# Clustered attention and an MLP on one core: row maxima over both halves of the keys at once, and PSUM divided anew

## The chip, the cores and the metric

The kernel runs on one core of a Trainium2 chip. A core has a matrix engine (TensorE, PE in the profile; PEld is its loading of weights), a vector engine (VectorE, DVE), a scalar engine (ScalarE, ACT), a general one (GpSimd, POOL) and queues for transfers (SP issues most of them, ScalarE's queue a few). Each engine takes its instructions in the order of the program and waits on semaphores. TensorE writes to PSUM, which has eight banks of 512 fp32 numbers for each of the 128 partitions, and VectorE and ScalarE read it there.

The metric is the device time of one execution in microseconds (us). Of the kernel before there are three runs, with a median of 1025.03 us (1023.77 to 1026.52). About 0.3% of that, 3.1 us, is what such a measurement can tell from no change.

## The reference

Attention within clusters for 4 batches and 8 heads, 768 positions of 64 numbers, then a mixing of positions of rank 32 and an MLP (512 to 2048 to 512), each with its residual:

```python
q_assign = np.argmax(np.einsum('bhsd,hcd->bhsc', q_n, c_n), axis=-1)
k_assign = np.argmax(np.einsum('bhsd,hcd->bhsc', k_n, c_n), axis=-1)
mask = q_assign[:, :, :, None] == k_assign[:, :, None, :]
scores = scale * np.matmul(q, k.transpose(0, 1, 3, 2))
scores = np.where(mask, scores, -1000000000.0)
scores = scores - np.max(scores, axis=-1, keepdims=True)
attn = np.exp(scores)
attn = attn / (np.sum(attn, axis=-1, keepdims=True) + 1e-09)
x = np.matmul(attn, v)            # heads side by side: (4, 768, 512)
...
xt = x.transpose(0, 2, 1)
h = xt @ U @ V
u = x + h.transpose(0, 2, 1)
ch = np.maximum(u @ w_ch1, 0.0) @ w_ch2
return (u + ch).astype(np.float32)
```

## The kernel before

Heads are worked in pairs: 16 of them (4 of each batch), j being the head within the pair. For a pair, queries and keys lie with their dimensions over the partitions, split into a high part (`X1`) and the rest (`X2`), so that two matmuls in a fast format give the accuracy of fp32. Below them stand 32 rows with the clusters, scaled so that a query and a key of different clusters get a huge negative score.

Stages of a pair:

- `load`, `split_hi`, `split_lo`, `place_*`: the transfers in, the split, and rows copied to the partitions where they are needed.
- `sims`, `largest`, `clusters`, `clusters_T`, `place_clusters`: similarities to the centroids (the tile `ps_sim`, turned into `ps_simT`), the largest of each row found on VectorE in five instructions that work in `ps_simT` itself, and the result turned (`ps_oh`) and placed.
- `rowmax`: for each unit u of 12 (a head and 128 queries), the scores of the high part against all 768 keys, in two halves h of 384. Each half is one matmul into a single bank (`ps_max`, L462) and one reduction on VectorE (L464) into a column of `m2`. `rowmax_T` (L469) takes the larger of the two halves for six or twelve units. `rowmax_place` turns the maxima (`ps_mT`), negates them on ScalarE (`mT`) and sends them by ScalarE's queue to a row of the queries' second part (row 96 of `X2`), where the matmul subtracts them.
- `scores`: for each of 12 steps (a half of the queries and 128 keys), four matmuls into the two banks of one tile `st`, one for each head (L500 with the high parts, L502 with the rest and the maxima), and one exponential over both (`pr`, L505).
- `weights`: the sums over keys, step by step, on GpSimd and some on VectorE (`T`, L515). `values`: six steps make a block of 12 matmuls (24 in the trace, which shows each of these in two) into one bank (`o_ps`, L523), which ScalarE copies out (`os`, L527).
- `sums`, `sums_T`, `normalise`: the sums over partitions, turned, and the outputs turned (`ps_oT`, L556) and divided.

After each four pairs `mix_u`, `mix_sum` and `mix_v` add the mix of positions (`mix_v`: one matmul into a bank named `ps_h`, L585, one addition on VectorE, L586, for each of six tiles). Beside all that, `load_weights` brings the weights, which come as 64-bit numbers, and joins them to fp32 on VectorE (L174 to L186; for the first two groups of them with a bank `ps_t` as the place of work). After the last pair the MLP runs in eight parts of 384 positions and 16 steps: `gemm1` (12 matmuls into `ps_h`), `gemm2` (9 into the three banks `y`).

The order is written out. `at(time, ...)` notes each piece of work with a time; times count in steps, 12 to a pair, and a piece's time is 12 i plus a number of the table `times`, with columns for most pairs, the last of a batch, the last, the first, the second and the third; `order0` holds those of the first pieces, and `spots` where the row maxima of six units stand within six steps. All are sorted by time and written in that order, which each engine keeps (`keep_order`). Which piece of a pool a tile gets follows from that order too; a tile waits until the one before it in its place has been read.

PSUM before: the pool `ps_w` has four single banks for everything short (`work`), the pool `ps_st` two tiles of two banks for the scores (and in the beginning for turned clusters). When the MLP begins, the four banks of `ps_st` become those of `y`.

Of the kernel before, what the change touches and what calls it, by code (L numbers as in the profile page):

```python
# [29 lines left out]
F32 = mybir.dt.float32  # L30
# [6 lines left out]
AX = mybir.AxisListType  # L37
# [16 lines left out]
GV = 6  # L54
# [5 lines left out]
    "load0":           (-34.72, -34.25, -43.39,   None,   None,  -24.6),  # L60
    "load1":           (-26.03, -29.07, -30.74,   None,   None,  -22.8),
    "sims":            ( -25.1, -28.59, -28.44,   None,   None, -21.52),
    "clusters_T":      (-19.38, -19.11, -17.83,   None, -12.09,  -13.9),
    "place_clusters":  (-18.31, -16.49, -15.63,   None, -10.17, -12.11),
    "split_hi0":       (-29.17, -30.23, -24.29,   None,   None, -20.71),
    "split_lo0":       (-24.63, -24.44, -24.29,   None,   None, -18.43),
    "split_hi1":       (-23.89, -23.69, -24.34,   None,   None, -19.53),
    "split_lo1":       (-23.65, -20.17, -23.57,   None,   None, -17.17),
    "place_keys_hi":   (-20.09, -23.65, -23.59,   None,   None, -17.07),
    "place_keys_lo":   (-19.84, -19.93, -21.77,   None,   None, -16.98),  # L70
    "place_queries":   (-16.28, -16.19, -18.28,   None,   None, -16.28),
# [5 lines left out]
    "scores":          (     0,  -0.97,  -0.37,  -0.47,   0.82,   0.95),
    "weights":         (  1.19,  -0.22,   0.44,   2.06,   2.71,   1.67),
    "values":          (  1.38,   1.51,   0.02,   0.68,   3.05,   1.52),
    "sums":            ( 14.31,  14.69,  13.43,   14.3,  15.51,  15.14),  # L80
    "sums_T":          ( 16.16,   16.1,   14.3,  15.86,   16.6,   16.3),
    "normalise0":      ( 18.83,  16.88,  14.88,   22.3,  20.85,  23.08),
    "normalise1":      ( 21.59,  17.72,  15.28,  26.53,  23.84,  19.17),
    "largest":         (-23.05, -22.46, -20.54,   None,   None, -21.24),
    "clusters":        ( -21.3, -22.34, -20.12,   None,   None, -18.18),
# [4 lines left out]
    "mix_u":    ( 18.88,  18.35,  18.81,  16.57),  # L90
    "mix_sum":  ( 19.25,  19.13,   19.1,   18.6),
# [5 lines left out]
    "mix":  (  4.41,   7.02,  11.43,  15.04,  16.45,  17.16),  # L97
    "g0":   ( 35.66,  38.22,  41.05,  42.54,  42.54,  51.82),
    "g1":   (-26.11, -21.73, -21.07,  -20.5,  -20.5, -18.35),
    "g2":   ( -2.37,  -1.41,  -0.87,  -0.74,  -0.75,  -0.21),  # L100
    "g3":   (  5.27,   6.49,   6.53,   7.36,   7.03,   8.06),
}


order0 = [-71, -70, -69, -65.96, -68.07, -66, -65.55, -64.02, -62.25, -62, -59.19, -60, -59.25, -58, -57, -56, -54.34, -57.1, -48.95, -51.97, -51, -50, -49, -48.11, -47, -46.37, -45, -44, -43.32, -42.29, -41, -40, -39, -38, -37, -35.81, -35, -34, -32.98, -31.86, -31.19, -32.6, -26.45, -27.88, -22.71, -25.79, -25, -21.96, -23.88, -22, -20.92, -22.82, -18.9, -18, -17, -15.66, -15, -14.07, -12.87]

spots = [0.6, 0.25, 1.8, 2.25, 1.26, 2.09, 2.97, 3, 3.49, 3.81, 4.72, 5.03]


def keep_order(tc, first=0):  # L110

# [677 lines left out]
```

## Time and profile before

| what | us |
| --- | --- |
| median of three runs | 1025.03 |
| the profiled execution | 1025.6 |
| its span, first to last instruction | 1023.5 |
| first values block starts | 44.97 |
| last values block starts | 462.55 |
| first matmul of the MLP starts | 468.34 |
| the maxima's reductions on VectorE, L464, 384 of them | 195.4 busy |
| the exponentials on ScalarE, L505, 192 of them | 154.8 busy |

Two views by time help with the rest. A stretch of the span is given with each engine's busy time, and with the clock granted to TensorE. A timeline lists instructions with their start and length, and in brackets how long the engine had been idle and which instruction released it. In names a number is left out: `ps_max` is any of those tiles, and `m` in a reduction's row is any of `m` and `m2`. Matmuls overlap, so that the start of the next one says more than a length: in the chain of waits two of 384 columns take 0.35 us, and a block of values 4.02.

### The profile page before, as it was taken

The numbers are of one execution on the slowest core, as the hardware profiler recorded it, in microseconds if no ns is written. First come the engines' busy times: TensorE is split into PE (matmuls) and PEld (weight loads), VectorE is DVE, ScalarE is ACT, GpSimd is POOL, SyncE is SP. The second block draws the span as 40 slices with busy tenths as digits, with TensorE's granted clock in tenths as the row PEclk, the third lists the DMA queues.
The fourth block names the chain that finished last, engine by engine and source line by source line (L and its number), as shares of the span: only waits on it lengthen the run. The fifth ranks groups of instructions, "written<-read, shape, count | busy, mean of one in ns | idle before, by whom it ended". The sixth has DMA issues, their size and how long they took to land.

```text
span 1023.5 us, 13820 instructions
## 1 busy us (share of the span) xinstructions
PE 999.9 (98%) x5419; PEld 796.3 (78%) x5419; DVE 488.9 (48%) x914; ACT 350.6 (34%) x573; POOL 361.8 (35%) x246
## 2 busy tenths in 40 slices
PE   7989999999999999989999999999999999999998
PEld 5566666676667666647889989999899899998997
DVE  5797777777877767777672121121121211211211
ACT  4454555565655545554441111111111111111110
POOL 5466677889788967744240000000000000000000
PEclk9999999999999999989999999999999999999999
DMA  6755554656475546143531001010010010100000
GB/s 164 190 132 128 145 148 104 199 156 156 108 207 139 125 109 180 58 131 107 188 111 63 1 4 59 1 62 1 1 62 1 2 61 1 62 1 1 31 1 31
DMA packets 28675, 87.71 MB, mean 86 GB/s; under 512 B 4874, under 2 KB 9476, under 8 KB 28100
## 3 DMA queue, kind: packets, MB, share of 16 engines
q1 hardware_dynamic: 28240, 86.76, 30.2%
q8 instruction: 42, 0.69, 0.3%
q14 instruction: 21, 0.17, 0.1%
q10 hardware_dynamic: 372, 0.10, 0.0%
HBM read 42.99 MB, written 12.58 MB: 54 GB/s over the span
## 4 chain that ended last, share of the span: by engine, by line
PE 90%; DVE 5%; ACT 1%; issue 1%; DMA 1%; POOL 1%; ACTq 0%; SPq 0%; DVEq 0%; POOLq 0%
PE o_ps L523 12%; PE ps_h L629 9%; PE ps_h L631 9%; PE ps_h L630 9%; PE y L647 9%; PE y L646 9%; PE y L645 9%; PE ps_max L462 7%; PE st L500 6%; PE st L502 6%; DVE m L464 2%; PE ps_sim L352 1%; PE ps_sum L535 1%; PE ps_uT L618 1%; PE ps_oT L556 1%
## 5 line engine op out<-in xcount | busy, mean ns | idle before, releaser
L515 POOL TENSOR_TENSOR T<-T,pr 128x768 f32<-128x768 f32 x120 | 228.1, 1901 | 48.9 <-ACT pr L505 20.5
L635 DVE SCALAR_TENSOR_TENSOR hl<-ps_h,hh 128x384 fp32r<-128x384 f32 x128 | 71.3, 557 | 360.9 <-ACT hh L634 360.9
L464 DVE TENSOR_REDUCE m<-ps_max 128x1 f32<-128x384 f32 x384 | 195.4, 547 | 85.4 <-PE ps_max L462 83.5
L634 ACT ACTIVATE hh<-ps_h 128x384 fp32r<-128x384 f32 x128 | 62.9, 492 | 381.3 <-PE ps_h L631 381.3
L505 ACT ACTIVATE pr<-st 128x768 f32<-128x768 f32 x192 | 154.8, 811 | 81.2 <-PE st L502 63.3
L523 PE MATMUL o_ps<-pr,vt 128*64 128x384 f32 x768 | 133.7, 499 | 0.0
L462 PE MATMUL ps_max<-arena 128*128 128x384 f32 x384 | 125.8, 376 | 7.7 <-ACT sims L355 2.4
L646 PE MATMUL y<-w2l,hh 128*128 128x512 f32 x288 | 113.6, 395 | 0.0
L500 PE MATMUL st<-arena 128*128 128x384 f32 x384 | 106.0, 357 | 1.8 <-ACT pr L505 1.8
L523 PEld LDWEIGHTS o_ps<-pr,vt 128*64 128x64 f32 x768 | 53.2, 139 | 68.0 <-issue 62.8
L462 PEld LDWEIGHTS ps_max<-arena 128*128 128x128 f32 x384 | 70.3, 191 | 44.5 <-issue 17.9
L502 PE MATMUL st<-arena 97*128 97x384 f32 x384 | 100.4, 343 | 2.9 <-DMA arena<-mT 2.7
L500 PEld LDWEIGHTS st<-arena 128*128 128x128 f32 x384 | 66.3, 191 | 17.7 <-issue 9.9
L515 POOL TENSOR_TENSOR T<-pr 128x768 f32<-128x768 f32 x30 | 56.4, 1881 | 60.7 <-ACT pr L505 60.7
L647 PE MATMUL y<-w2h,hl 128*128 128x512 f32 x192 | 76.1, 396 | 0.0
L647 PE MATMUL y<-arena,hl 128*128 128x512 f32 x192 | 76.0, 396 | 0.0
L645 PE MATMUL y<-w2h,hh 128*128 128x512 f32 x192 | 75.1, 391 | 0.0
L645 PE MATMUL y<-arena,hh 128*128 128x512 f32 x192 | 74.8, 390 | 0.0
L502 PEld LDWEIGHTS st<-arena 97*128 97x128 f32 x384 | 71.1, 192 | 3.9 <-issue 2.8
L646 PEld LDWEIGHTS y<-w2l,hh 128*128 128x128 f32 x288 | 54.0, 188 | 9.1
L527 ACT COPY os<-o_ps 128x384 f32<-128x384 f32 x32 | 15.3, 479 | 106.5 <-PE o_ps L523 106.5
L629 PE MATMUL ps_h<-arena,w1h 128*128 128x384 f32 x128 | 44.7, 350 | 0.2 <-DVE arena L621 0.2
(138 smaller groups left out, 1614.7 us busy)
## 6 DMA issues: line engine op xcount, KB each, us to landing
rw<-in_w SPq DMA_DIRECT2D x32, 512.0 KB
R<-in_qk SPq DMA_DIRECT2D x32, 384.0 KB
arena<-arena SPq DMA_DIRECT2D x32, 384.0 KB
arena<-arena SPq DMA_DIRECT2D x64, 192.0 KB
vt<-in_v SPq DMA_DIRECT2D x16, 384.0 KB
u_scr<-xt SPq DMA_DIRECT2D x4, 1536.0 KB
u<-u_scr SPq DMA_DIRECT2D x8, 768.0 KB
out_y<-u SPq DMA_DIRECT2D x24, 256.0 KB
```

The lines of the kernel that those rows point to most:

```text
L462: nc.tensor.matmul(ps[:, 0:HS], x1[:, 0, g // 2, g % 2, t * P:(t + 1) * P], x1[:, 1, h, g % 2, :], start=True, stop=True)
L464: nc.vector.reduce_max(live["m2", i][:, h, u:u + 1], ps[:, 0:HS], axis=AX.X)
L500: nc.tensor.matmul(st[:, j, 0:HS], x1[:, 1, hk, j, ks], x1[:, 0, h, j, :], start=True, stop=False)
L502: nc.tensor.matmul(st[:, j, 0:HS], x2[0:97, 1, hk, j, ks], x2[0:97, 0, h, j, :], start=False, stop=True)
L505: nc.scalar.activation(pr, st[:, :, 0:HS], AF.Exp, scale=SCALE)
L515: eng.tensor_add(T, live["p", i, h, 0] if c == 1 else T, live["p", i, h, c])
L523: nc.tensor.matmul(o_ps[64 * j:64 * j + 64, 0:HS], vv[:, c, j, :], pr[:, j, :], start=(c == 0), stop=(c == NT - 1))
L629: nc.tensor.matmul(ps[:, 0:HS], w1h[:, d, fs], uh[:, d, :], start=(d == 0), stop=False)
L630: nc.tensor.matmul(ps[:, 0:HS], w1h[:, d, fs], ul[:, d, :], start=False, stop=False)
L645: nc.tensor.matmul(y[t], hh[:, ts], w2h[:, f % FG, :], start=(f == 0), stop=False)
L646: nc.tensor.matmul(y[t], hh[:, ts], w2l[:, f % FG, :], start=False, stop=False)
L647: nc.tensor.matmul(y[t], hl[:, ts], w2h[:, f % FG, :], start=False, stop=(f == NF - 1))
```

## The change

`rowmax` puts the matmuls of the two halves into the two banks of one tile `st`, and one reduction over both axes gives the maximum over all keys; `rowmax_T` and `m2` are gone. The pool `ps_st` has three double tiles, which scores, row maxima and turned clusters take in turn, and `ps_w` two single banks for all the rest. In the MLP, the six banks of `ps_st` become the four of `y` and two more single ones, and `gemm1` takes its bank from the two pools in turn.

```diff
-    ps_w = ctx.enter_context(tc.tile_pool(name="ps_w", bufs=4, space=PSUM, side="right"))
+    ps_w = ctx.enter_context(tc.tile_pool(name="ps_w", bufs=2, space=PSUM, side="right"))
...
-    ps_st = early.enter_context(tc.tile_pool(name="ps_st", bufs=2, space=PSUM))
+    ps_st = early.enter_context(tc.tile_pool(name="ps_st", bufs=3, space=PSUM))
...
-    def rowmax(i, u, *halves):
+    def rowmax(i, u):
...
-        if ("m2", i) not in live:
-            live["m2", i] = sb.tile([P, 2, 2 * NT], F32, name="m2")
-        for h in halves or range(2):
-            ps = work("ps_max")
-            nc.tensor.matmul(ps[:, 0:HS], x1[:, 0, g // 2, g % 2, t * P:(t + 1) * P],
+        if ("m", i) not in live:
+            live["m", i] = sb.tile([P, 2 * NT], F32, name="m")
+        ps = ps_st.tile([P, 2, 512], F32, name="st")
+        for h in range(2):
+            nc.tensor.matmul(ps[:, h, 0:HS], x1[:, 0, g // 2, g % 2, t * P:(t + 1) * P],
                              x1[:, 1, h, g % 2, :], start=True, stop=True)
-            nc.vector.reduce_max(live["m2", i][:, h, u:u + 1], ps[:, 0:HS], axis=AX.X)
-
-    def rowmax_T(i, u0, u1):
-
-        m = live["m", i, u0] = sb.tile([P, 2 * NT], F32, name="m")[:, 0:u1 - u0]
-        nc.vector.reduce_max(m, live["m2", i].rearrange("p h u -> p u h")[:, u0:u1], axis=AX.X)
+        nc.vector.reduce_max(live["m", i][:, u:u + 1], ps[:, :, 0:HS], axis=AX.XY)
...
+        pool["w"] = ctx.enter_context(tc.tile_pool(name="ps_w2", bufs=2, space=PSUM, reuse_waits="tile"))
         pool["y"] = ctx.enter_context(tc.tile_pool(name="ps_y", bufs=4, space=PSUM, reuse_waits="tile"))
...
-        ps = work("ps_h")
+        ps = (pool["w"] if f % 2 else ps_w).tile([P, 512], F32, name="ps_h", tag="w")
```

The tables are new in many places, mostly by less than half a step; two rows of them:

```diff
-    "rowmax":          (-14.88, -14.94,  -14.8, -12.18,  -8.11, -10.78),
-    "rowmax_place":    ( -2.26,  -2.27,  -2.48,   0.84,   2.29,  -0.17),
+    "rowmax":          (-14.88, -14.94,  -14.8, -12.45,  -8.11, -10.78),
+    "rowmax_place":    ( -2.26,  -2.27,  -2.48,   1.43,   2.29,  -0.01),
...
-spots = [0.6, 0.25, 1.8, 2.25, 1.26, 2.09, 2.97, 3, 3.49, 3.81, 4.72, 5.03]
+spots = [0.6, 1.8, 1.27, 2.97, 3.16, 4.72]
```

In the first pair the turned row maxima of six units now go ahead of the second pair's `largest`.

What this does to the order is seen at three places. Line numbers after the change are smaller by one at the reductions (L463) and by six at the scores (L494, L496); the row maxima's matmuls are L461. The first place is VectorE during the second pair's row maxima (the pair whose maxima are in `m2_510` before and in `m_481` after). Before:

```order
L464 TENSOR_REDUCE m2_510<-ps_max_611 128x1
L464 TENSOR_REDUCE m2_510<-ps_max_614 128x1
L469 TENSOR_REDUCE m_619<-m2_510 128x6
L464 TENSOR_REDUCE m2_510<-ps_max_621 128x1
L464 TENSOR_REDUCE m2_510<-ps_max_624 128x1
L515 TENSOR_TENSOR T_634<-pr_546,pr_580 128x768
```

And after:

```order
L463 TENSOR_REDUCE m_481<-st_575 128x1
L463 TENSOR_REDUCE m_481<-st_579 128x1
L509 TENSOR_TENSOR T_590<-pr_512,pr_544 128x768
L463 TENSOR_REDUCE m_481<-st_592 128x1
L463 TENSOR_REDUCE m_481<-st_608 128x1
```

Two reductions have become one, and the fold of the halves is gone. The second place is TensorE after the end of the first batch, behind the turn of the eighth pair's similarities (`ps_simT`). Before:

```order
L362 MATMUL ps_simT_1969<-ident_84,sims_1830 128x128 x3
L462 MATMUL ps_max_1979<-arena_97 128x384
L500 MATMUL st_1982<-arena_97 128x384 x2
L502 MATMUL st_1982<-arena_97 128x384 x2
L462 MATMUL ps_max_1989<-arena_97 128x384
L535 MATMUL ps_sum_1996<-T_1668,sel_120 32x384 x2
L535 MATMUL ps_sum_1996<-T_1847,sel_120 32x384 x2
L500 MATMUL st_2003<-arena_97 128x384 x2
L502 MATMUL st_2003<-arena_97 128x384 x2
L462 MATMUL ps_max_2011<-arena_97 128x384
L462 MATMUL ps_max_2014<-arena_97 128x384
```

And after:

```order
L361 MATMUL ps_simT_1799<-ident_84,sims_1674 128x128 x3
L461 MATMUL st_1809<-arena_97 128x384 x2
L494 MATMUL st_1813<-arena_97 128x384 x2
L496 MATMUL st_1813<-arena_97 128x384 x2
L529 MATMUL ps_sum_1824<-T_1522,sel_120 32x384 x2
L529 MATMUL ps_sum_1824<-T_1687,sel_120 32x384 x2
L494 MATMUL st_1831<-arena_97 128x384 x2
L496 MATMUL st_1831<-arena_97 128x384 x2
L461 MATMUL st_1839<-arena_97 128x384 x2
```

The halves of a row maximum, which stood apart, stand together, and their tiles no longer come from the pool that holds `ps_simT`. The third place is VectorE in the MLP's first part, where three matmuls of `mix_v` for the last batch stand together on TensorE and their additions (L586, after the change L580) on VectorE behind a join of weights. Before:

```order
L181 TENSOR_SCALAR rw_t_5315<-rw_g_5289 128x512
L186 SCALAR_TENSOR_TENSOR rw_t_5315<-rw_5251,rw_t_5315 128x512
L183 SCALAR_TENSOR_TENSOR rw_t_5315<-rw_g_5289,rw_t_5315 128x512
L586 TENSOR_TENSOR xt_4436<-ps_h_5330,xt_4436 128x512
L586 TENSOR_TENSOR xt_4436<-ps_h_5333,xt_4436 128x512
L586 TENSOR_TENSOR xt_4436<-ps_h_5336,xt_4436 128x512
```

And after:

```order
L180 TENSOR_SCALAR rw_t_4898<-rw_g_4896 128x512
L182 SCALAR_TENSOR_TENSOR rw_t_4898<-rw_g_4896,rw_t_4898 128x512
L580 TENSOR_TENSOR xt_4049<-ps_h_4910,xt_4049 128x512
L580 TENSOR_TENSOR xt_4049<-ps_h_4913,xt_4049 128x512
L580 TENSOR_TENSOR xt_4049<-ps_h_4916,xt_4049 128x512
L185 SCALAR_TENSOR_TENSOR rw_t_4898<-rw_4832,rw_t_4898 128x512
```

One instruction of the join has moved behind the additions, whose three tiles now come from two banks.

In the last pair, the order on TensorE from the last row maximum to the turn of the maxima was row maximum, scores, turn; it is row maximum, two scores tiles, turn. In two places a turn of the outputs (L556, after the change L550) directly follows a values block and takes the bank of that very block, once it is copied out.

More of the change, by code (lines that the diff above doesn't have):

```diff
@@ L74 @@
-    "rowmax":          (-14.88, -14.94,  -14.8, -12.18,  -8.11, -10.78),
-    "rowmax_T":        ( -3.08,  -3.31,  -3.73,  -3.18,   0.32,  -2.19),
-    "rowmax_place":    ( -2.26,  -2.27,  -2.48,   0.84,   2.29,  -0.17),
[L77 to L85, printed above, removed]
+    "load0":           (-34.72, -35.03, -43.85,   None,   None,  -24.6),
+    "load1":           (-25.78, -29.13, -30.74,   None,   None, -24.24),
@@ new lines @@
+    "sims":            ( -25.1, -28.59, -29.99,   None,   None, -21.52),
+    "clusters_T":      (-19.38, -18.44, -17.83,   None, -12.09,  -13.9),
+    "place_clusters":  (-18.31, -16.49, -15.63,   None, -10.17, -12.64),
+    "split_hi0":       (-29.11, -30.23, -24.29,   None,   None, -19.88),
+    "split_lo0":       (-24.63, -24.44, -24.17,   None,   None, -18.43),
+    "split_hi1":       (-23.89, -23.69, -24.34,   None,   None, -19.53),
+    "split_lo1":       (-23.74,  -20.1, -23.78,   None,   None, -17.17),
@@ new lines @@
+    "place_keys_hi":   (-20.09, -23.32, -23.59,   None,   None, -17.07),
+    "place_keys_lo":   (-19.31, -19.85, -21.77,   None,   None, -16.81),
+    "place_queries":   (-15.06, -16.19, -18.28,   None,   None, -16.49),
+    "place_ones":      (-14.51, -12.46,  -8.56,   None,   None, -21.44),
+    "load_v":          (-19.47,   -6.3,  -8.13,   None, -21.51,  -8.69),
+    "rowmax":          (-14.88, -14.94,  -14.8, -12.45,  -8.11, -10.78),
+    "rowmax_place":    ( -2.26,  -2.27,  -2.48,   1.43,   2.29,  -0.01),
@@ new lines @@
+    "scores":          (     0,  -1.01,   0.02,  -0.47,   0.82,   0.95),
+    "weights":         (  1.19,  -0.22,   0.44,   2.06,   2.71,   2.06),
+    "values":          (  1.38,   1.51,   0.02,   0.68,   3.05,   1.39),
+    "sums":            ( 14.31,  14.69,  13.43,  13.85,  15.54,  15.14),
+    "sums_T":          ( 16.16,   16.1,  14.01,  15.86,   16.6,   16.3),
+    "normalise0":      ( 18.83,  17.82,  14.88,   21.6,  20.85,  23.16),
+    "normalise1":      ( 21.59,  17.72,  15.65,  26.53,  24.27,  19.17),
@@ L86 @@
+    "largest":         (-23.05, -22.42, -20.54,   None,   None,  -21.2),
+    "clusters":        ( -21.3, -22.34, -19.71,   None,   None, -18.18),
 }
 mixes = {
-    "mix_u":    ( 18.88,  18.35,  18.81,  16.57),
-    "mix_sum":  ( 19.25,  19.13,   19.1,   18.6),
+    "mix_u":    ( 18.88,  18.35,  18.37,   16.7),
+    "mix_sum":  ( 19.14,  19.13,   19.1,   18.6),
     "mix_v":    (  20.5,   20.4,  20.66,  19.42),
@@ L487, in rowmax_place @@
         ps = work("ps_mT")
-        nc.tensor.transpose(ps[0:u1 - u0, 0:P], live.pop(("m", i, u0)), ident)
+        nc.tensor.transpose(ps[0:u1 - u0, 0:P], live["m", i][:, u0:u1], ident)
         mT = sb.tile([2 * NT, P], F32R, name="mT")[0:u1 - u0]
@@ L704, in clustered_attention_moe @@
         for u in range(NT if i == 0 else 0, NS):
-            for h in range(2):
-                if i < 3:
-                    at(when("rowmax", i) + pace * u + 0.01 * h, rowmax, i, u, h)
-                else:
-                    g, r = divmod(2 * u + h, 2 * GV)
-                    at(when("rowmax", i) + GV * g + spots[r], rowmax, i, u, h)
+            if i < 3:
+                at(when("rowmax", i) + pace * u, rowmax, i, u)
+            else:
+                g, r = divmod(u, GV)
+                at(when("rowmax", i) + GV * g + spots[r], rowmax, i, u)
         if i == 1:
-            at(when("rowmax_T", i) - 4, rowmax_T, i, 0, NT)
             at(when("rowmax_place", i) - 5, rowmax_place, i, 0, NT)
         u0 = NT if i < 2 else 0
-        at(when("rowmax_T", i), rowmax_T, i, u0, NS)
         at(when("rowmax_place", i), rowmax_place, i, u0, NS)
```

29 lines of the change are left out of this document (8 added, 21 removed).

## The prediction

> **What bounds the kernel now.** I read the page first, then the chain of waits, then the busy times by stretch.
>
> The page gives the span, each engine's busy time, the shares of the chain that ended last, and the group of row-maximum reductions:
>
> ```profile
> span 1023.5 us, 13820 instructions
> PE 999.9 (98%) x5419; PEld 796.3 (78%) x5419; DVE 488.9 (48%) x914; ACT 350.6 (34%) x573; POOL 361.8 (35%) x246
> PE 90%; DVE 5%; ACT 1%; issue 1%; DMA 1%; POOL 1%; ACTq 0%; SPq 0%; DVEq 0%; POOLq 0%
> L464 DVE TENSOR_REDUCE m<-ps_max 128x1 f32<-128x384 f32 x384 | 195.4, 547 | 85.4 <-PE ps_max L462 83.5
> ```
>
> TensorE is 90% of the chain, VectorE 5%. The change adds and removes no matmul, so it can only move the tenth that isn't TensorE, about 100 us at most, and much of that is the start-up. The stretches show where VectorE sits in it (columns: start and end, their length, busy us of PE, PEld, DVE, ACT, POOL, granted clock, DMA share, GB/s):
>
> ```profile
> 29.00:34.00 5.00, 4.34 (x10) 2.30 (x11) 5.00 (x12) 0.00 (x0) 0.00 (x0) 0.91 0.93 247
> 45.00:78.00 33.00, 30.40 (x176) 20.43 (x178) 30.03 (x58) 17.74 (x27) 22.36 (x12) 1.00 0.61 149
> 78.00:125.00 47.00, 45.15 (x260) 29.84 (x257) 34.83 (x66) 22.73 (x33) 28.10 (x17) 0.96 0.51 132
> 200.00:250.00 50.00, 50.00 (x310) 34.59 (x308) 38.04 (x75) 29.66 (x45) 44.77 (x26) 1.00 0.59 157
> 300.00:350.00 50.00, 49.88 (x308) 34.29 (x307) 35.27 (x71) 29.26 (x44) 45.55 (x25) 1.00 0.57 150
> 426.00:448.00 22.00, 18.43 (x87) 10.09 (x86) 15.21 (x24) 8.96 (x15) 13.19 (x8) 0.84 0.51 174
> 500.00:507.00 7.00, 7.00 (x36) 6.24 (x35) 6.70 (x12) 2.13 (x4) 1.30 (x1) 1.00 0.34 97
> ```
>
> At 29-34 VectorE never rests and at 45-78 it is 91% busy while TensorE waits: it is the bound there. At 200-250 and 300-350 TensorE is busy throughout: a cheaper reduction buys nothing. From about 475 us on only the two matrix products of the MLP run.
>
> **The cheaper reduction.** Two reductions of 384 elements become one of 768 from two banks, which the trace doesn't show. The nearest rows are VectorE runs of several instructions, and the means of single ones:
>
> ```profile
> 183.52 1.94 DVE L464 TENSOR_REDUCE m<-ps_max 128x1 f32<-128x384 f32 x4
> 505.77 1.88 DVE L586 TENSOR_TENSOR xt<-ps_h,xt 128x512 f32<-128x512 f32 x3
> L586 DVE TENSOR_TENSOR xt<-ps_h,xt 128x512 f32<-128x512 f32 x24 | 16.0, 682 | 3.6 <-PE ps_h L585 3.5
> L469 DVE TENSOR_REDUCE m<-m 128x12 f32<-128x24 f32 (+1 forms) x18 | 3.1, 174 | 0.5
> ```
>
> Back to back 384 elements take 0.485 us (1.94/4) and 512 take 0.627 (1.88/3), 1.11 ns an element, so 768 take 0.91 against 0.97 for the two: 0.06 saved. By the means (547 and 682 ns, 1.05 ns an element) 768 take 0.95 against 1.09: 0.14 saved. I take 0.10 a unit, between them. The fold of the two halves (0.174 us) goes as well. All 192 units and 18 folds make about 22 us of VectorE time, and what counts is where it is waited for:
>
> ```profile
> L464 DVE TENSOR_REDUCE m<-ps_max 128x1 f32<-128x384 f32 x38 | 19.1, 547 | 2.5 <-PE ps_max L462 2.1
> L464 DVE TENSOR_REDUCE m<-ps_max 128x1 f32<-128x384 f32 x22 | 10.6, 547 | 2.7 <-PE ps_max L462 2.6
> L464 DVE TENSOR_REDUCE m<-ps_max 128x1 f32<-128x384 f32 x39 | 19.7, 547 | 11.0 <-PE ps_max L462 10.8
> ```
>
> The first row is 45-78 us: 19 units by 0.10, and 3 folds, **-2.4 us** (-1.1 to -3.2). The second is 20-36: 11 units and 2 folds, **-1.4** (-0.7 to -1.9). The third is 78-125, where VectorE is busy for 74%: of 19.5 units by 0.10 I count a third, **-0.7** (0 to -1.9). Elsewhere nothing, since TensorE's own work hides it.
>
> The Trainium skill ("VectorE: DVE Perf Modes", section on the TRN2 errata) prices a VectorE instruction from PSUM at 120 cycles plus one per element, at 0.96 GHz. By that 384 elements take 525 ns, near the row's 547, and 768 take 925, an estimate that saves 0.125 a unit; with it the first term would be -2.9 us in place of -2.4.
>
> **The banks.** A row maximum no longer takes two of four single banks, among which it stood behind tiles that VectorE holds for long (the similarities, weights being joined). These idle times of TensorE before a row maximum are all of that kind:
>
> ```profile
> 183.66 0.44 PE L462 MATMUL ps_max<-arena 128*128 128x384 f32 x1 [0.33 <-DVE oh L378]
> 289.49 0.44 PE L462 MATMUL ps_max<-arena 128*128 128x384 f32 x1 [0.33 <-DVE oh L378]
> 396.98 0.45 PE L462 MATMUL ps_max<-arena 128*128 128x384 f32 x1 [0.44 <-DVE m L464]
> 398.74 0.58 PE L462 MATMUL ps_max<-arena 128*128 128x384 f32 x2 [0.62 <-DVE rv L545]
> 424.93 0.91 PE L462 MATMUL ps_max<-arena 128*128 128x384 f32 x2 [0.92 <-DVE rw_t L177]
> ```
>
> They add up to 2.64 us, of which I take **-1.8** (0 to -2.6): VectorE is as late as before for what comes next. The scores get a third double bank; what they wait for now is an exponential that has not emptied one of two:
>
> ```profile
> PEld st L500 <- ACT pr L505: 5.5, 16, 1.7
> PE st L500 <- ACT pr L505: 1.8, 2, 1.4
> 437.16 0.62 PE L500 MATMUL st<-arena 128*128 128x384 f32 x2 [1.41 <-ACT pr L505]
> ```
>
> That is 7.3 us, of which 1.41 stands before a longer wait for a transfer; of the other 5.9 I take **-2.5**, because weight loads can wait beside a running matmul and row maxima now use the third bank too.
>
> **What it costs.** The single banks are two, not four. Three matmuls of the mix stand together (L585, 500.45 and 505.32 us); the third now waits until VectorE has added the first one:
>
> ```profile
> 500.45 0.87 PE L585 MATMUL ps_h<-x,v 96*128 96x512 f32 x3
> 505.32 0.87 PE L585 MATMUL ps_h<-x,v 96*128 96x512 f32 x3
> L527 ACT COPY os<-o_ps 128x384 f32<-128x384 f32 x32 | 15.3, 479 | 106.5 <-PE o_ps L523 106.5
> L389 ACT ACTIVATE ohT<-ps_oh,obi,osc 128x768 fp32r<-128x768 bf16 x15 | 14.9, 992 | 0.1
> 237.04 0.35 PE st L500 x2
> 236.23 0.18 PE ps_max L462
> ```
>
> The first is there after 0.49 us (0.87 less the two others' 0.19 each), its addition takes 0.68, and the third would have started after 0.38: 0.8 us each time, **+1.6** (0 to 2.2, with the product behind it). TensorE is busy all of 500-507, so it is not hidden. In two places a turn of the outputs (L556) stands directly behind a block of values and needs the bank that ScalarE still copies (0.48 us); before, the next matmul started at once: I count 0.5 each, **+1.0** (0 to 1.2).
>
> The last cost is the ring itself. Row maxima (two matmuls, 0.36 us) and scores (four, 0.70) take three double banks in turn, so a late reduction holds up scores and a late exponential holds up row maxima. Behind the turned clusters ScalarE has 0.99 us and then the exponentials of 0.81 each. The row maximum that needs the first of these banks is issued 0.36 + 0.70 + 0.70 = 1.76 us later, against 0.99 + 0.81 = 1.80; up to 0.45 with a part of a 0.6 us weight cast before. Over 12 pairs that is 0 to 5.4; I take **+1.0**.
>
> Sum: -2.4 - 1.4 - 0.7 - 1.8 - 2.5 + 1.6 + 1.0 + 1.0 = -5.2 us. The profiled execution took 1025.6 us (2.1 outside its span), so 1020.4; the median is 0.6 below that execution: **1019.8 us**. The moves in the table are mostly under half a step; the transfers on SP keep their order but for neighbours that swap, and I cost them at nothing behind 50 to 60% DMA share.
>
> **The rivals.**
>
> *The clock (1015 us).* Before the last pair's first values TensorE waits for the row of maxima, and the next block runs slow:
>
> ```profile
> 439.75 0.98 PE L502 MATMUL st<-arena 97*128 97x384 f32 x2 [1.97 <-DMA arena<-mT]
> 440.65 6.77 PE L523 MATMUL o_ps<-pr,vt 128*64 128x384 f32 x24
> 453.05 4.09 PE L523 MATMUL o_ps<-pr,vt 128*64 128x384 f32 x24
> ```
>
> The clock in 426-448 is 0.84. If the maxima leave earlier (no fold, and two scores tiles stand between the last row maximum and their turn), half of the 3.4 us of waits goes, and with it the slow block: 1.7 + 2.7 + 0.5 = 4.9 more, 1014.9. Against it: ScalarE's row of work ahead of that transfer stays as it is.
>
> The Trainium skill ("TensorE: Matmul & The Clock Gate", "What's actually happening") has the clock halved after an idle window of about 3.4 us. The trace agrees, with 1.41 and 1.97 us of waits ahead of the slow block; by that rule a slightly shorter wait would save the whole of it.
>
> *Hidden anyway (1024 us).* Either the reduction over two banks costs as much as two, or VectorE waits for something else in 45-78. Then the first three terms go to -0.8 (folds) and the sum to -1.5, 1024.1 on the profiled execution, about 1024. For it: TensorE is busy throughout at 200-250 and 300-350, most of the pairs.
>
> *Slower (1029 us).* The ring decides: from 0.45 us a pair on, 5.4 us of new waits meet a third bank that is worth nothing. Sum: -4.5 for VectorE, -0.9 for the banks, 0 for the scores, +1.6 +1.2 +5.4 = +2.8, 1028.4 on the profiled execution; with a few more early waits 1029. Against it: at 200-250 VectorE is busy for only 76%, and the order after puts scores together and row maxima just before the values, where 4 us pass.
>
> **How the numbers follow.** Forecast 0.45, clock 0.17, hidden 0.24, slower 0.14. Under 0.3% (3.1 us) a measurement can't tell from no change. Below 1022: 0.40 of the forecast's 0.45 and the clock, 0.57; the rest of it and the hidden case, 0.29; slower 0.14. All gains at their far ends and no cost give -15 us, 1010; all costs and the least gains give +7.0. The range is 1010 to 1029, which leaves out most of the slow tail.
>
> **What would show it.** VectorE's busy time falls by 25 to 31 us, and one reduction of 768 takes 0.90 to 0.96 us. In 45-78 TensorE's busy share rises. Row maxima no longer wait for the similarities. Two new waits stand at the mix near 500 us. New waits of scores for a reduction, in most pairs, would make the slower case; a wait for the transfer under 2 us with a values block of 4.1 us behind it, the clock's.

## The result, and the profile after

The changed kernel takes **1038.7 us** (median of four runs, 1037.5 to 1041.38) against 1024.4 us before (1023.22 to 1026.52): a ratio of 1.0141, 95% interval 1.0113 to 1.0169. (The runs of before are four here; three of them made the median of 1025.03 above.) It is 14.3 us slower; the forecast was 5.2 us faster. Its profiled span is 1036.0 us against 1023.5, 12.5 more, and that is what the traces can be asked about.

The page of the changed kernel, in the order of the lines of before:

```profile
span 1036.0 us, 13632 instructions
PE 998.3 (96%) x5419; PEld 788.6 (76%) x5419; DVE 478.4 (46%) x704; ACT 348.7 (34%) x573; POOL 363.7 (35%) x246
PE 89%; ACT 4%; DVE 4%; DMA 1%; POOL 1%; issue 1%; ACTq 0%; DVEq 0%; POOLq 0%
L463 DVE TENSOR_REDUCE m<-st 128x1 f32<-128x768 f32 x192 | 177.9, 952 | 42.3 <-PE st L461 40.1
```

TensorE's work is the same (998.3 against 999.9 us), so all of the difference is time in which it stands: 37.7 us of the span, 23.6 before. ScalarE has grown on the chain from 1% to 4%: TensorE now waits for exponentials. Where it stands is read from a mark that both kernels have, ScalarE's copy of each of the 32 blocks of values. Four of these copies before (the 4th, 9th, 24th and 31st) and the ninth ReLU of the MLP, by their start:

```profile
98.47 0.48 ACT L527 COPY os<-o_ps 128x384 f32<-128x384 f32 x1 [3.31 <-PE o_ps L523]
162.31 0.48 ACT L527 COPY os<-o_ps 128x384 f32<-128x384 f32 x1 [3.46 <-PE o_ps L523]
361.17 0.48 ACT L527 COPY os<-o_ps 128x384 f32<-128x384 f32 x1 [2.85 <-PE o_ps L523]
457.19 0.48 ACT L527 COPY os<-o_ps 128x384 f32<-128x384 f32 x1 [2.12 <-PE o_ps L523]
508.31 0.49 ACT L634 ACTIVATE hh<-ps_h 128x384 fp32r<-128x384 f32 x1 [2.93 <-PE ps_h L631]
```

And the same five in the changed kernel:

```profile
95.94 0.48 ACT L521 COPY os<-o_ps 128x384 f32<-128x384 f32 x1 [3.16 <-PE o_ps L517]
161.07 0.48 ACT L521 COPY os<-o_ps 128x384 f32<-128x384 f32 x1 [3.78 <-PE o_ps L517]
365.29 0.48 ACT L521 COPY os<-o_ps 128x384 f32<-128x384 f32 x1 [3.47 <-PE o_ps L517]
465.82 0.48 ACT L521 COPY os<-o_ps 128x384 f32<-128x384 f32 x1 [3.50 <-PE o_ps L517]
520.82 0.49 ACT L629 ACTIVATE hh<-ps_h 128x384 fp32r<-128x384 f32 x1 [2.38 <-PE ps_h L626]
```

The changed kernel is 2.5 us ahead at the 4th block, 1.2 ahead at the 9th, 4.1 behind at the 24th, 8.6 behind at the 31st and 12.5 behind in the MLP; from there on the lag stays at 12.5. So there are three losses. **In the pairs** (9th to 24th block) it loses 5.4 us, mostly in steps of 0.4 to 0.6. **At the 31st block** it loses 4.2 at once. **At the start of the MLP** it loses 3.7 to 3.9. A smaller one lies before them: of the 2.5 us that it is ahead at the 4th block, 1.4 go at the 5th, 0.58 of them in a turn of the outputs (96.48 us) that waits until its own values block has been copied out.

TensorE's waits between the 9th and the 24th block, in the changed kernel (who waits for whom, total us, times, longest):

```profile
PE st L461 <- ACT pr L499: 1.5, 6, 0.3
PE st L494 <- ACT pr L499: 1.2, 2, 0.6
PE st L496 <- DMA arena<-mT: 0.9, 1, 0.9
PE st L494 <- DVE m L463: 0.6, 2, 0.3
```

And in the kernel before, all there is:

```profile
PE ps_max L462 <- DVE oh L378: 0.7, 2, 0.3
```

Row maxima (L461) wait for exponentials, and scores (L494) for exponentials and for reductions: each stands behind the reader of a double bank that the other may have held. These three come to 3.3 us, the late transfer to 0.9; what else makes up the 5.4 us is not seen as a wait of a matmul. At the end the waits have other names. The last pair's values wait for VectorE to read the turned sums of pair 14; the second pair of turns of u and the third matmul of each triple of the mix wait for VectorE too (the other triple's, at 517.83 us, for 0.55 us again):

```profile
459.04 0.87 PE L517 MATMUL o_ps<-pr,vt 128*64 128x384 f32 x4 [2.84 <-DVE rv L539]
477.08 1.19 PE L613 MATMUL ps_uT<-ident,u 128*128 128x128 f32 x6 [0.52 <-DVE arena L616]
512.12 0.49 PE L579 MATMUL ps_h<-x,v 96*128 96x512 f32 x1 [0.55 <-DVE xt L580]
```

These tiles all come from the pool of single banks, which has two where it had four. The sums of pair 14 are turned at 455.71 us; VectorE reads them 3 us later, behind a join of weights and an addition of the sums over keys (`T`):

```profile
456.90 2.00 DVE L509 TENSOR_TENSOR T<-T,pr 128x768 f32<-128x768 f32 x1 [0.19 <-POOL T L509]
458.83 0.16 DVE L539 TENSOR_SCALAR rv<-ps_sumT 128x12 f32<-128x12 f32 x1
462.42 0.96 DVE L509 TENSOR_TENSOR T<-T,pr 128x768 f32<-128x768 f32 x1 [0.47 <-ACT pr L499]
```

The last row is the same addition 5.5 us later, in half the time. At 456.90 GpSimd was at work, until 458.10 us; at 462.42 it was not. The last section shows such a delay again.

The stretches 45-78, 200-250, 300-350 and 426-448 us in the changed kernel (columns as before):

```profile
45.00:78.00 33.00, 30.34 (x178) 20.24 (x176) 26.95 (x36) 17.49 (x26) 21.71 (x12) 1.00 0.60 143
200.00:250.00 50.00, 49.54 (x305) 33.45 (x305) 35.02 (x49) 29.18 (x44) 43.38 (x24) 1.00 0.58 157
300.00:350.00 50.00, 49.54 (x302) 34.13 (x300) 35.03 (x48) 30.11 (x44) 43.29 (x25) 1.00 0.57 151
426.00:448.00 22.00, 17.07 (x92) 11.41 (x92) 19.19 (x26) 12.63 (x20) 18.26 (x11) 0.96 0.36 108
```

At 45-78 VectorE has come down from 30.03 to 26.95 us and TensorE hasn't gained (30.40, now 30.34). The waits of TensorE in this stretch say why. Before:

```profile
PE ps_sum L535 <- ACT mT L490: 0.7, 1, 0.7
PE ps_max L462 <- ACT sums L537: 0.6, 1, 0.6
PE ps_max L462 <- DVE m L464: 0.6, 2, 0.3
PE ps_oh L387 <- DVE m L464: 0.5, 1, 0.5
PE ps_mT L488 <- DVE m L464: 0.2, 1, 0.2
```

And in the changed kernel:

```profile
PE st L461 <- ACT pr L499: 1.9, 3, 1.0
PE st L494 <- ACT pr L499: 0.7, 2, 0.5
```

It waited 2.6 us, half of them for VectorE; it waits 2.6 us still, all of them for an exponential that holds a double bank. The relief is there, and the shared ring of double banks takes its place. The changed kernel was 1.8 us ahead at the first values block already, and 2.0 at the third. At 200-250 and 300-350 TensorE, which was busy without a break, now rests about 0.5 us in 50.

### The profile page after: what moved, and what is told of

It is laid out like the page before. It is cut to its first block, busy times and chain, and to the rows that moved or that the text cites. A ratio compares the mean times of both kernels' runs of the same rounds, so it can differ in the third digit from the quotient of the medians.

```text
span 1036.0 us, 13632 instructions
## 1 busy us (share of the span) xinstructions
PE 998.3 (96%) x5419; PEld 788.6 (76%) x5419; DVE 478.4 (46%) x704; ACT 348.7 (34%) x573; POOL 363.7 (35%) x246
## 4 chain that ended last, share of the span: by engine, by line
PE 89%; ACT 4%; DVE 4%; DMA 1%; POOL 1%; issue 1%; ACTq 0%; DVEq 0%; POOLq 0%
PE o_ps L517 13%; PE ps_h L624 9%; PE ps_h L626 9%; PE ps_h L625 9%; PE y L642 9%; PE y L641 9%; PE y L640 8%; PE st L494 6%; PE st L461 6%; PE st L496 5%; ACT pr L499 2%; DVE m L463 2%; PE ps_oT L550 1%; PE ps_sim L351 1%; PE ps_uT L613 1%
## 5 line engine op out<-in xcount | busy, mean ns | idle before, releaser
L463 DVE TENSOR_REDUCE m<-st 128x1 f32<-128x768 f32 x192 | 177.9, 952 | 42.3 <-PE st L461 40.1
L494 PE MATMUL st<-arena 128*128 128x384 f32 x384 | 108.5, 364 | 5.6 <-ACT pr L499 2.9
L461 PE MATMUL st<-arena 128*128 128x384 f32 x384 | 104.7, 365 | 6.5 <-ACT pr L499 4.6
L496 PE MATMUL st<-arena 97*128 97x384 f32 x384 | 99.9, 341 | 4.5 <-DMA arena<-mT 4.4
L494 PEld LDWEIGHTS st<-arena 128*128 128x128 f32 x384 | 63.6, 190 | 31.7 <-issue 13.7
L461 PEld LDWEIGHTS st<-arena 128*128 128x128 f32 x384 | 63.7, 190 | 27.9 <-ACT pr L499 10.4
L496 PEld LDWEIGHTS st<-arena 97*128 97x128 f32 x384 | 70.4, 190 | 5.7 <-DMA arena<-mT 3.4
```

Source lines behind the costliest of these rows:

```text
L461: nc.tensor.matmul(ps[:, h, 0:HS], x1[:, 0, g // 2, g % 2, t * P:(t + 1) * P], x1[:, 1, h, g % 2, :], start=True, stop=True)
L463: nc.vector.reduce_max(live["m", i][:, u:u + 1], ps[:, :, 0:HS], axis=AX.XY)
L494: nc.tensor.matmul(st[:, j, 0:HS], x1[:, 1, hk, j, ks], x1[:, 0, h, j, :], start=True, stop=False)
L496: nc.tensor.matmul(st[:, j, 0:HS], x2[0:97, 1, hk, j, ks], x2[0:97, 0, h, j, :], start=False, stop=True)
```

## The experiments

Two theories at first. **Ring**: scores and row maxima share three double banks and hold each other up; this makes the loss in the pairs. **Two single banks**: these make the losses at the end. Rivals: the new placing (the table) is at fault; the joins of weights, which hold single banks, make the loss in the pairs as well. This table has each kernel's time, that of the runs of before beside it, and the lag of its profiled execution against the profile of before at the five marks (minus is ahead). In late13 and hyb4 the profiled execution is a short one, 1029.2 and 1029.5 us, so that their lags are smaller than their times:

| kernel | us | before | 4th | 9th | 24th | 31st | MLP |
|---|---|---|---|---|---|---|---|
| changed | 1038.7 | 1024.4 | -2.5 | -1.2 | +4.1 | +8.6 | +12.5 |
| mlp4 | 1035.7 | 1023.7 | -1.7 | -0.8 | +5.6 | +8.1 | +10.0 |
| sumT | 1034.2 | 1023.7 | -1.1 | 0.0 | +5.5 | +4.4 | +8.2 |
| oldtab | 1046.0 | 1023.7 | +0.1 | +3.7 | +9.2 | +12.0 | +18.6 |
| two2 | 1047.5 | 1024.4 | +3.8 | +5.8 | +13.0 | +18.8 | +22.6 |
| own2 | 1064.2 | 1024.4 | +11.9 | +15.3 | +26.3 | +34.5 | +38.8 |
| late13 | 1031.1 | 1024.4 | -0.5 | -0.1 | +3.6 | +3.9 | +3.9 |
| hyb4 | 1031.4 | 1024.4 | -0.5 | +0.3 | +3.7 | +4.1 | +4.1 |
| ring2b | 1104.2 | 1024.3 | -1.8 | +10.6 | +57.6 | +77.4 | +78.1 |
| hyb4b | 1028.5 | 1024.3 | -1.2 | +0.1 | +3.9 | +4.0 | +4.0 |
| hyb3b | 1027.8 | 1024.3 | +0.2 | +0.6 | +2.9 | +1.6 | +1.6 |
| joinsb | 1052.8 | 1024.4 | +4.4 | +5.5 | +11.7 | +18.9 | +28.5 |
| fixall | 1048.1 | 1024.4 | +4.3 | +5.2 | +9.9 | +17.6 | +24.0 |
| bjoin | 1035.2 | 1024.4 | +0.2 | +0.3 | +3.2 | +9.4 | +9.8 |

Up to the 24th block the changed kernel, mlp4 and sumT have the same code. Their lags there differ by up to 1.5 us, and what they lose from the 9th to the 24th block is 5.4, 6.4 and 5.6 us; smaller differences mean nothing.

### mlp4: four single banks again, in the MLP alone

```diff
     def work(name):
-        return ps_w.tile([P, 512], F32, name=name, tag="w")
+        turn[0] += 1
+        return (pool["w"] if "w" in pool and turn[0] % 2 else ps_w).tile([P, 512], F32, name=name, tag="w")
```

The first product takes its bank from `work`, too.

> The changed kernel, but from the opening of the MLP on all single tiles (the turns of u, the mix, the first product) take four banks in turn, as before the change. Theory 'two single banks': the 1.5 us at the turns of u and the 2.0 us at the two triples of the mix go, 1038.7 becomes about 1035.2, and the first products of the MLP stand 9 us behind the kernel before instead of 12.5. Rival 'VectorE is late there anyway (joins of weights)': the waits stay, within 1 us of 1038.7.

Measured: 1035.72 us, ratio to before 1.0117 (1.0097 to 1.0137). The 2.0 us at the triples are gone: the three matmuls of the mix run as one group again.

```profile
510.40 0.87 PE L582 MATMUL ps_h<-x,v 96*128 96x512 f32 x3
```

The waits of the turns of u stay. In this kernel, too, all four turns come ahead of the point where the MLP's banks open, so they still have two; the edit missed them, and of the 3.5 us expected 2.0 were to be had.

### sumT: the turned sums of pair 14 in a double bank

```diff
-        ps = work("ps_sumT")
+        ps = ps_st.tile([P, 2, 512], F32, name="st")[:, 0] if i == 14 else work("ps_sumT")
```

> The changed kernel, but the turned sums of pair 14 stand in a double tile of the scores and not in a single bank. Theory 'two single banks': the last pair's first block of values no longer waits 2.84 us for VectorE to read the sums; about 3 us less, 1035.7, if nothing else takes the place of that wait. Rival 'hidden anyway': the values wait for their last exponentials or the transfer of the maxima at that place, 1038 to 1039; or the ring is held by the sums instead, and the scores behind them wait 2 us.

Measured: 1034.16 us, ratio 1.0097 (1.0077 to 1.0116). The step from the 30th to the 31st block was +4.2 us and is +0.3: the single bank was what the values waited for, and the wait cost more than its 2.84 us, since TensorE ran slowly behind it (granted clock 0.91 at 448-476). These are the changed kernel's scores and values right behind that wait; two such scores take 0.62 us at 465.70:

```profile
459.84 0.93 PE L494 MATMUL st<-arena 128*128 128x384 f32 x2
460.56 0.84 PE L496 MATMUL st<-arena 97*128 97x384 f32 x2
461.34 0.91 PE L517 MATMUL o_ps<-pr,vt 128*64 128x384 f32 x2
```

### oldtab: the changed banks with the old placing

The tables `times`, `mixes`, `stages`, `order0` and `spots` of before stand in the changed kernel, without a use of the fold and with one spot to a unit.

> The changed kernel with the times, stages, spots and the order of the start of before the change. Theory 'the table is at fault': most of the 14 us goes, under 1030. Theories 'ring' and 'two single banks': the loss stays, 1036 to 1046, since the banks are what is waited for.

Measured: 1046.04 us, ratio 1.0222 (1.0202 to 1.0241), 7.3 us slower than the changed kernel. The new placing is not at fault; with these banks it is worth some 7 us. From the 9th to the 24th block the old one loses 5.5 us, as the new one does, and the ring's waits there are 1.7, 1.2 and 0.6 us, for 1.5, 1.2 and 0.6.

### two and two2: the cheaper reduction undone

Both put two reductions of 384 and the fold in the place of one of 768 and keep banks and placing. In `two` each reduction stands behind its own matmul, in `two2` both stand behind both matmuls:

```diff
-        nc.vector.reduce_max(live["m", i][:, u:u + 1], ps[:, :, 0:HS], axis=AX.XY)
+        for h in range(2):
+            nc.vector.reduce_max(live["m2", i][:, h, u:u + 1], ps[:, h, 0:HS], axis=AX.X)
```

> The changed kernel with two reductions of 384 (one of each bank of the double tile) and a fold of the halves, as before the change; banks and placing are the changed ones. It prices the cheaper reduction alone. As forecast (0.10 us a unit and the folds where VectorE is the bound): 4.5 us slower than the changed kernel, 1043.2. If only the 2.2 us gained up to the fourth block of values is its work: 1041. If it is hidden: 1039. If two reductions free their banks so late that the ring of three doubles stalls in most pairs: 1045 or more.

> The changed kernel with two reductions of 384 for each unit, issued behind both of its matmuls, and the fold of the halves; banks and placing are the changed ones. It prices the cheaper reduction alone. As forecast (0.10 us a unit and the folds, where VectorE is the bound): 4.5 us slower than the changed kernel, 1043. Rival 'hidden, the ring of doubles is waited for in any case': within 1 us of it. If a longer hold of the doubles feeds the ring: 3 to 8 us more between the ninth and the 24th block of values, 1045 or more.

`two` took 1305.74 us, ratio 1.2765 (1.2738 to 1.2793): it measured something else. The two halves are one tile, and the second half's matmul waited until the first half's reduction had read that tile, as a row on TensorE shows (the last matmul of a unit at 302.55 us):

```profile
302.55 0.44 PE L462 MATMUL st<-arena 128*128 128x384 f32 x1 [0.94 <-DVE m L464]
```

`two2` took 1047.46 us, ratio 1.0225 (1.0208 to 1.0243), 8.8 us slower than the changed kernel. So in these banks the cheaper reduction is worth 8.8 us, twice what was forecast for it; that a double bank is held for a shorter time is part of this, and isn't told apart. The time is the third case's (1045 or more), the place is not: some 6 of the 8.8 us are there at the 4th block, and from the 9th to the 24th `two2` loses 7.2, only 1.8 more than the changed kernel, with the same waits in the ring (1.5, 1.2 and 0.6 us). `two2` also says what the banks and the new placing together cost the first pairs: with the same reductions as before the change it lags by 3.8 us at the 4th block and 5.8 at the 9th. The saving is real, and the banks take it away again.

### own2: row maxima in two single banks of their own

Row maxima by halves and a fold, from a pool of their own; scores have two doubles, the rest two singles.

```diff
-    ps_st = early.enter_context(tc.tile_pool(name="ps_st", bufs=3, space=PSUM))
+    ps_st = early.enter_context(tc.tile_pool(name="ps_st", bufs=2, space=PSUM))
+    ps_m = early.enter_context(tc.tile_pool(name="ps_m", bufs=2, space=PSUM))
```

> Row maxima by halves again, with two reductions and a fold, but in two single banks of their own; scores have two doubles to themselves, all other work two singles. Placing is the changed one. Theory 'ring' (row maxima and scores hold each other up): the 5.4 us lost between the ninth and the 24th block of values go, to within 1 us, while the losses of the last pairs (some 4 us) and of the MLP's start (3.7 us) stay; 1033 to 1036, with 0 to 3 us for the dearer reductions in the first pairs. Rival 'two single banks are short in every pair': the loss between those blocks stays at 4 us or more, 1038 or more.

Measured: 1064.24 us, ratio 1.0387 (1.0368 to 1.0406), and 11.0 us lost between the 9th and the 24th block. The ring's forecast (1033 to 1036) missed. The rival's came by its words (4 us or more, 1038 or more), but by another wait than it had named: with two banks a row maximum waits for the reduction of the one before the last (3.4 us of TensorE's waits in those pairs, none of that kind before). So it doesn't tell the theories apart.

### late13: four single banks from pair 13 on

At the start of pair 13's row maxima the third double is closed and opened as two singles; from there on row maxima go by halves, with the old times.

```diff
+    def narrow():
+        wide.close()
+        ps_x[:] = None, ctx.enter_context(tc.tile_pool(name="ps_x1", bufs=2, space=PSUM, side="right"))
```

> The changed kernel up to pair 12; from pair 13 on the third double bank is two single ones, row maxima go by halves into the four singles, with the times of the kernel before. Both theories: the creep between the ninth and the 24th block stays as it is (5.4 us). Theory 'two single banks': the losses of the last pairs and of the MLP's start (8.4 us) go, 1030 to 1031. Rival 'VectorE and ScalarE are behind by then, whatever the banks': at most 3 us go, 1036 or more.

Measured: 1031.05 us, ratio 1.007 (1.0056 to 1.0085). Up to the 24th block it loses 3.7 us from the 9th, behind it no more than 0.3 us. So the 8.4 us at the end belong to the last pairs and the MLP's start as the change has them. late13 takes back banks, halves and times there all at once; that it is the single banks is shown for 5.9 us, by sumT (3.9) and mlp4 (2.0), and argued for the rest.

### hyb4, hyb4b, hyb3b: the change in the first pairs alone

Three doubles and fused reductions for the first four pairs (hyb3b: three), then banks, halves and times of before. In hyb4 the four singles are two pools in turn; in the other two they are one:

```diff
+    def narrow():
+        wide.close()
+        singles[0] = ctx.enter_context(tc.tile_pool(name="ps_w4", bufs=4, space=PSUM, side="right"))
+        doubles[0] = early.enter_context(tc.tile_pool(name="ps_st2", bufs=2, space=PSUM))
```

> Fused reductions and three doubles for pairs 0 to 3 alone; from pair 4 on the banks, the halves and the times of before the change (its mixes and weight stages throughout). Theories 'ring' and 'two single banks' together: the creep and the losses of the end go, and what is left is the gain of the first pairs, -1 to -2 us against the kernel before, 1022 to 1023.5. If the forecast's 4.5 us for VectorE had been right and only the banks cost: 1019.5 to 1020.5. If the table or the fused start is at fault: 1026 or more.

> As the fourth kernel of the last set (three doubles and fused reductions for pairs 0 to 3 alone, then banks, halves and times of before), but the four singles are one pool, so that a single that is free is taken past one that is held, as before the change; there they were two pools taken in turn. If the 3.3 us lost there between the ninth and the 24th block came from the two pools taken in turn: they go to within 1 us, and it comes out at 1023 to 1026. If they came from the changed first pairs (a shift of transfers and of VectorE's work that the table was not made for): they stay, 1030 to 1032.

> The same, but only pairs 0 to 2 have three doubles and fused reductions. The gain of the change in the first four blocks of values (2.0 to 2.5 us) is kept if the loss behind it (1.4 us at the fifth block) comes from three doubles in the fourth pair: 1021.5 to 1023. If that loss is the price of the earlier start (the maxima's transfer, late by then): 1023.5 to 1026.

Measured: hyb4 1031.39 us, ratio 1.0076 (1.0055 to 1.0097); hyb4b 1028.51, 1.004 (1.0024 to 1.0055); hyb3b 1027.75, 1.0034 (1.0021 to 1.0047). None beats the kernel before. hyb4 came out where its third case stood, the table or the fused start at fault (1026 or more); hyb4b lies between its two cases, and hyb3b above both of its. hyb4b still loses 3.8 us in the pairs. But it loses them otherwise. These are its waits between the 9th and the 24th block:

```profile
PE st L549 <- DMA arena<-mT: 3.4, 4, 1.4
PE ps_max L501 <- DVE oh L417: 0.6, 2, 0.3
```

No row maximum waits for an exponential and no score for a reduction any more. At the blocks where the changed kernel steps by 0.25, 0.64, 0.38 and 0.43 us (the 10th to the 13th), hyb4b steps by 0.01, 0.04, 0.82 and -0.01, and the 0.82 is one of four transfers of maxima that come late. That one is issued 0.14 us later than before the change (196.86 us, 196.72 before), and the transfers ahead of it on SP stand in the same order at the same distances; yet the matmul that needs it starts at 200.56, behind a wait, where it started at 199.68 without one. So the transfer takes longer, and why isn't settled. Without the shared ring, then, the ring's 3.3 us of waits are gone, and all but 1.6 of the 5.4 us are still lost. The gain of the first pairs is not kept in any of the three.

### ring2b: two doubles for scores and fused row maxima

From pair 4 on as hyb4b, but row maxima stay fused and share the two doubles with the scores, with the changed placing.

> The changed kernel up to pair 3; from pair 4 on scores and fused row maxima share two doubles, and the other work has one pool of four singles. Theory 'ring': two doubles for both hold each other up much more than three; from the ninth to the 24th block of values at least 15 us more than before the change, while the losses of the last pairs and of the MLP's start (8.4 us) go. Rival 'two singles are short in every pair': the 5.4 us of the changed kernel in those blocks go, to within 1 us, and the whole comes out near 1024.

Measured: 1104.21 us, ratio 1.0781 (1.0759 to 1.0802). From the 9th to the 24th block it loses 47 us, 3.1 a block, with four single banks at hand. Of its waits in the pairs (162 to 380 us) these are the three longest:

```profile
PE st L502 <- ACT pr L507: 9.4, 18, 0.6
PE st L469 <- ACT pr L507: 7.9, 15, 1.0
PE st L469 <- DVE m L471: 4.9, 8, 1.1
```

They are the waits of the changed kernel, grown: scores and row maxima behind exponentials, and row maxima behind reductions. Three doubles for both are better than two.

### joinsb, fixall, bjoin: the joins' place of work in SBUF

```diff
-            b = work("ps_t").bitcast(I32)[0:r, 0:n]
+            b = raw.tile([P, 512], I32, name="rw_b", bufs=1)[0:r, 0:n]
```

joinsb is the changed kernel with this edit; fixall has mlp4's, sumT's and a double bank for two turns of u as well; bjoin is the kernel before with it, and with one buffer instead of two for the largest similarities (`mx`).

> The changed kernel, but the place of work of the first weight joins (held by VectorE for 2 us each) is in SBUF, so that the two single banks are free of it. Theory 'ring' for the steady loss between the ninth and the 24th block of values: it stays at 4 us or more (transfer waits of 0.6 to 1.4 us apart); only the wait of 1.70 us before a turn of the outputs in the last pairs goes, 1036 to 1037.5. Rival 'two singles are short in every pair': the steady loss falls below 2 us, 1033 to 1035.

> The changed kernel with every loss at single banks removed that the trace names: the joins in SBUF, the turned sums of pair 14 and two turns of u in a double tile, four banks in turn in the MLP. Theories 'ring' and 'two single banks': 3.9 + 2.0 + 1.3 + 1.5 us less, 1029 to 1031, and what is left against the kernel before (5 to 6 us) is the loss in the pairs. If the loss in the pairs is the singles' too: 1024 to 1026.

> The kernel before with the joins' place of work in SBUF. Its trace has 1.5 us of waits of row maxima for a bank that a join holds (0.92 us at 425 among them): 1 to 1.5 us faster than before, 1023, if nothing else takes their place; no change if the same row maxima then wait for the next bank.

Measured: joinsb 1052.77 us, ratio 1.0278 (1.0264 to 1.0292); fixall 1048.08, 1.0236 (1.0222 to 1.025); bjoin 1035.21, 1.0113 (1.0099 to 1.0128). As times all three missed by 12 to 17 us, because steps of the joins came to take longer (last section) and VectorE was late with them. For the open question joinsb is clear all the same. Its waits in the pairs, with no join in a single bank:

```profile
PE st L461 <- ACT pr L499: 1.4, 6, 0.3
PE st L496 <- DMA arena<-mT: 1.4, 2, 0.8
PE st L494 <- ACT pr L499: 1.2, 2, 0.6
PE st L494 <- DVE m L463: 0.6, 2, 0.3
```

That is the changed kernel's list (1.5, 1.2 and 0.6), and its steps from the 10th to the 13th block are 0.25, 0.64, 0.40 and 0.42 us, the changed kernel's to 0.02. The waits in the ring aren't the joins' doing. They come to 3.1 to 3.5 us in every kernel that shares three double banks there, with either placing, either place of the joins, and fused or split reductions (`two`, whose matmuls wait inside a unit, apart), and they are gone in the three that don't share them. fixall's steps are the same (0.25, 0.64, 0.41, 0.42), and its MLP starts without the waits at the mix.

## Why the prediction was wrong

**The step that failed** is the third double bank: "The scores get a third double bank ... of the other 5.9 I take -2.5". It compared two doubles for the scores with three, but the three are for scores and row maxima, and each row maximum now holds two banks where a half held one. It set the gain of the third bank and the coupling of the ring (+1.0) side by side as two terms, where there is one balance. Measured, TensorE's waits for exponentials rose over the whole kernel from 1.8 us to 7.5, where the third bank was forecast to gain 2.5, and those of row maxima and scores for the reductions from 1.2 to 4.5:

```profile
PE st L461 <- ACT pr L499: 4.6, 13, 1.0
PE st L494 <- ACT pr L499: 2.9, 5, 1.0
PE st L494 <- DVE m L463: 2.7, 6, 0.8
PE st L461 <- DVE m L463: 1.8, 2, 1.5
```

Between the 9th and the 24th block the changed kernel loses 5.4 us, 3.3 of them in these waits and about 1.0 behind a late transfer. These waits are what holds TensorE there; what the ring costs net of what would take its place is a smaller figure, 1.6 us by hyb4b (traces of equal code differ by 1.0 there), since late transfers stand in their place. two2's 5.8 us by the 9th block is what banks and placing cost the first pairs; oldtab, 4.9 us later at that block than the changed kernel, speaks for the banks.

**The cheaper reduction** (-4.5) had its mechanism right and its size too small. One of 768 takes 952 ns on the mean, 0.14 below two of 547, the upper end of what was taken; its rows fall from 195.4 to 177.9 us, the fold's 3.1 go, and undoing it costs 8.8 us. That hardly shows in the first pairs since the ring took what VectorE gave (the waits at 45-78): 2.5 us ahead at the 4th block, 1.2 at the 9th, where 4.5 were forecast. The sign "VectorE's busy time falls by 25 to 31 us" was wrong, 10.5, and didn't fit the working either, which has about 22. Its rows fell by 20.6; but records of successive instructions overlap (the prediction's four reductions of 547 ns take 1.94 us), so rows don't add up to an engine's busy time. And "in 45-78 TensorE's busy share rises" was wrong, it stayed.

**Row maxima behind the similarities** (-1.8): these waits are gone, as said. They were the smaller evil: 2.64 us in all.

**The two single banks.** The triples of the mix cost 2.0 (forecast +1.6), and turns behind their own values block do wait, 0.6 us in the early and 0.6 in the last pairs (+1.0). What the step left out are two places of the same kind: the values behind the turned sums of pair 14 (4.2 us at the block, 3.9 by its removal) and the turns of u, four tiles in two banks (two waits of 0.52 us). A third, a turn of the outputs that waits 1.70 us for a join at 441.15, stands ahead of the last pair's wait for a transfer (2.08 us), so that its price isn't shown. I had searched for tiles that stand close together on TensorE; the sums of pair 14 hold their bank long not because TensorE needs it but because a join and an addition of 2.00 us, itself drawn out from 0.96, stand ahead of their reading on VectorE.

**The moves in the table** were costed at nothing. They are worth 7.3 us with these banks (oldtab).

**The rivals.** The slower case had the right mechanism, the ring in most pairs, and a chance of 0.14. That its 5.4 us are the figure lost between the 9th and the 24th block is luck: only 3.3 of these are waits in the ring there, and the waits are more often for exponentials than for the reductions that its sign named. It missed the end of the program, 8.4 us, and so gave 1029 where 1038.7 came. The hidden case was right in one thing: the relief of VectorE at 45-78 bought nothing, though not because VectorE had another wait. The clock's case: the transfer's wait in the last pair stayed (2.08 us against 1.97), the granted clock at 426-448 rose from 0.84 to 0.96, and the slow stretch moved behind the wait for the sums instead (0.91 at 448-476), behind one wait of 2.84 us, where the prediction had two, of 1.41 and 1.97, ahead of the slow block.

**What stays open**: what the three doubles and what the two singles cost the first pairs, each by itself; 2.5 of the 8.4 us at the end, which no run takes apart; and why transfers of maxima take longer in hyb4b's pairs, which decides how much of the 5.4 us there is the ring's.

## What to carry to other kernels

Count banks by who holds them and for how long, not by how many an operation gets: giving two users one larger ring put each behind the other's reader here, and a reduction over two banks holds both for all of its 0.95 us. When a pool shrinks, go through every tile of it and ask which engine frees it and what stands ahead of that reading in the engine's row; the costly one is a tile whose reader is late, wherever TensorE needs the bank next. A gain on the engine that seems to be the bound is to be checked by what TensorE waits for next: VectorE had 3 us less to do in 33, and TensorE was no earlier.

## What the runs showed of the hardware

A join's second step, 128x512 from SBUF with its place of work in PSUM, takes 695 ns in the changed kernel between 100 and 440 us, where GpSimd is busy for most of the time (262 of 340 us in joinsb); with the place of work in SBUF it takes 2027 ns on the mean in the same stretch (joinsb). First the changed kernel's row, then joinsb's:

```profile
L174 DVE SCALAR_TENSOR_TENSOR ps_t<-rw_g,ps_t 128x512 int32<-128x512 int32 x11 | 7.7, 695 | 0.4
```

```profile
L174 DVE SCALAR_TENSOR_TENSOR rw_b<-rw_g,rw_b 128x512 int32<-128x512 int32 x9 | 18.2, 2027 | 0.3
L182 DVE SCALAR_TENSOR_TENSOR rw_t<-rw_g,rw_t 128x512 int32<-128x512 int32 x6 | 4.2, 693 | 0.2
```

The last row is the same operation with both inputs in SBUF behind 540 us in joinsb, where GpSimd is busy for 11.8 of 500 us: 693 ns. So SBUF isn't slow by itself. Nor does the step run slowly beside GpSimd: it waits for it. Of the nine, eight take 2.19 us and one, with GpSimd at rest (141.79 us), 0.69. This is one of the eight, and GpSimd's additions beside it:

```profile
165.77 2.19 DVE L174 SCALAR_TENSOR_TENSOR rw_b<-rw_g,rw_b 128x512 int32<-128x512 int32 x1
161.70 5.71 POOL L509 TENSOR_TENSOR T<-T,pr 128x768 f32<-128x768 f32 x3
```

The step ends 0.55 us after the last of them (167.96 and 167.41), and so it does at 196.88 and 222.53; the join's next step, again with both inputs in SBUF, then takes 0.69 us. The Trainium skill ("SBUF — State Buffer", section "SBUF: two separate sides") has VectorE and GpSimd share a pair of ports that one instruction holds for its whole length, for a VectorE instruction with two inputs in SBUF against a GpSimd one that reads SBUF; the rows agree. PSUM was the right place for the joins, though it costs banks: in SBUF they cost the changed kernel 14.1 us (joinsb) and the kernel before 10.8 (bjoin).
